# Weight pieces of a fused linear-attention and feed-forward kernel: fetched ahead of the second token group, with two of their sums done by accumulating transfers

## The chip, the cores and the metric

The kernel runs on one core of one Trainium2 chip. The metric is device time in microseconds (us) of one execution; lower is better. Engines are named as the profile names them: PE (TensorE matmuls), PEld (its weight loads, which overlap PE), DVE (VectorE), ACT (ScalarE), POOL (GpSimd) and SP (SyncE, which here only issues transfers). Each engine works through its own list of instructions in order, and waits where an instruction's inputs aren't there yet. Transfers are issued from the queues of SP, ACT or POOL and carried by 16 DMA engines.

## The reference

A decayed linear attention over 768 tokens, 4 batches, 8 heads of width 48, whose output (3,072 tokens of 384 values) goes through a feed-forward network with an exact GELU. The feed-forward weights are float64, the rest float32.

```python
for t in range(S):                                   # attention, per batch and head
    state = alpha[:, :, t, :, None] * state + np.einsum('bhd,bhe->bhde', k[:, :, t], v[:, :, t])
    y[:, :, t] = np.einsum('bhd,bhde->bhe', q[:, :, t], state)
x = y.transpose(0, 2, 1, 3).reshape(B * S, H * D)    # 3072 x 384
h = x @ w_in                                         # 384 -> 2048
g = 0.5 * h * (1.0 + erf(h * inv_sqrt2))
out = g @ w_out                                      # 2048 -> 384
```

## The kernel before

**Groups and units.** The tokens are cut into 12 groups of 256. A group's attention is done in two units, each for four heads: unit (g, u) is half u of group g. For a unit, DVE scans the decays forward and multiplies q by them (`ahead`, lines 254 to 258), scans them backward and multiplies k (lines 265 and 268); PE makes the scores and turns k over (lines 284 and 293); DVE masks the scores (line 305), ACT copies the turned k out (`kn`, line 300); PE multiplies with v (lines 322 and 340); DVE adds four states in a row (lines 357 and 359); PE adds the part that comes through the states (line 384, "the outer part" below); ACT and then PE and ACT again (groups 0 to 2) or DVE (later groups) split the result into a high and a low part of x (lines 426, 435, 441, 430). The bank `ybank` that holds a unit's result exists once, so units follow each other through it. After a group's second unit, small transfers finish x (line 450).

**Feed-forward steps.** The 2,048 hidden values are cut into 8 slices f. Step (g, f) is one first product for group g (`hp`, line 458, 18 matmuls of 256 columns), two GELUs on ACT (lines 470 and 471), the low part of the GELU's result, and one second product (`acc`, line 497, 12 matmuls of 384 columns). The low part is a DVE subtraction (line 476), or, for groups 0 to 2 in the first part of the program, a matmul with a negative identity (line 480) and an ACT copy (line 484). There are 96 steps. When steps of another group follow, the sums leave PSUM into `part` (lines 511 to 515, on DVE).

**Weight pieces.** Slice f needs two pieces, number 2f of `w_in` and 2f + 1 of `w_out`; 16 in all, each 128x768. [...] In the order of a piece n: `u` on ACT (line 197), then on DVE four operations c0 to c3 (lines 201, 205, 215, 220), which leave the leading bits in `w` and the rest; c4 (line 230) adds the two; `hi` (line 233, ACT) rounds the sum to the matmul's format, and `lo` (line 236, DVE) is what the rounding left. Steps with slice f can start once hi and lo of both pieces are there.

**What sets the order.** Nothing is ordered by a scheduler at run time. The kernel holds a small planner: operations with assumed costs, dependencies and ranks are placed on a simulated clock, and the list sorted by start is then issued to every engine by hand. Two things feed it that the change touches: the string `ORDER`, which interleaves units (digits) and pieces (letters), and dependency lists such as that of a piece's fetch. Units and pieces therefore stand in fixed order in each engine's list, and a list stops where its next instruction must wait. SP fetches the loads of units and pieces in its own order. POOL holds only set-up, 18 multiplications of q (line 261, groups 3 to 11) and 11 output transfers (line 521).

The two lines of the kernel before that the change replaces by transfers are these:

```python
nc.vector.tensor_tensor(out=d["w"], in0=d["w"], in1=staged[n].bitcast(F32)[:, 1::2], op=ALU.add)      # c4
nc.vector.tensor_tensor(out=flat(lo), in0=d["w"], in1=flat(hi).bitcast(F32), op=ALU.subtract)         # lo
```

Of the kernel before, what the change touches and what calls it, by code (L numbers as in the profile page):

```python
# [20 lines left out]
STAGE = 3  # L21
# [4 lines left out]
UNTIL = 100.0  # L26
# [5 lines left out]
ORDER = "0 1 2 3 a b c d e f 4 5 g h i j k l m n o p"  # L32
# [3 lines left out]
def gla_then_gelu_ffn(ctx: ExitStack, tc: tile.TileContext, q, k, v, alpha, qg, kg, ag, w_in, w_out, out):  # L36
# [154 lines left out]
    def conversion(n):  # L191
# [3 lines left out]
        def scaled():  # L195
            d["u"] = stage.tile([P, 2 * DM], F32, tag="u", bufs=1, name=f"u_{n}")
            nc.scalar.activation(d["u"], staged[n].bitcast(F32)[:, 1::2], AF.Copy, scale=2.0**-112)
# [5 lines left out]
        def signed():  # L203
            d["w"] = stage.tile([P, 2 * DM], F32, tag="w", bufs=2, name=f"w_{n}")
# [14 lines left out]
        def rest():  # L219
            nc.vector.scalar_tensor_tensor(  # L220
                out=staged[n].bitcast(F32)[:, 1::2],
# [7 lines left out]
        def whole():  # L229
            nc.vector.tensor_tensor(out=d["w"], in0=d["w"], in1=staged[n].bitcast(F32)[:, 1::2], op=ALU.add)  # L230

        def high():
            nc.scalar.copy(flat(hi), d["w"])

        def low():
            nc.vector.tensor_tensor(out=flat(lo), in0=d["w"], in1=flat(hi).bitcast(F32), op=ALU.subtract)
# [255 lines left out]
    def gemm2(g, f, ghi, glo, acc, first, last, done, n0=None):  # L492
        for k in range(2):
            for t in range(2):
                for j in range(2):
# [11 lines left out]
        def evacuate():
            o = parts[0 if g == "s" else g % NSB]
            for t in range(2):
                if g in started:  # L510
                    nc.vector.tensor_tensor(out=o[:, t], in0=o[:, t], in1=acc[t], op=ALU.add)
                elif t == 1 and g == NG - 1:
# [3 lines left out]
                if g == NG - 1:  # L516
                    nc.sync.dma_start(out[g * G + t * C : g * G + (t + 1) * C, :], o[:, t])
# [124 lines left out]
    def plan_unit(n):  # L642
# [11 lines left out]
        d["load"] = op("SP", "load", lambda: load_data(g, u), [old.get("outer"), old.get("scores"), old.get("c0"), old.get("c1")] + ([unit[n - NB * NU].get("inside")] if old else []), rank=r - 30, lands=2.8)  # L654
# [13 lines left out]
        if g < NSB:  # L668
# [25 lines left out]
    def plan_piece(n):  # L694
# [234 lines left out]
```

## Time and profile before

| | us |
|---|---|
| three runs | 543.62, 539.23, 541.49 |
| their median | 541.49 |
| the profiled execution's own time | 538.57 |
| its span in the profile | 537.0 |

| engine | busy us | share of the span |
|---|---|---|
| PE | 511.0 | 95% |
| PEld | 495.7 | 92% |
| DVE | 302.4 | 56% |
| ACT | 210.1 | 39% |
| POOL | 38.6 | 7% |

The span is 1.6 us shorter than the execution's time. The page cuts the span into 40 slices of 13.4 us and gives the busy share of each in tenths; a shares-of-the-span table hides what these show, that PE and DVE are bound in different parts of the program:

```
PE   6667899999999999999999999999999999999995
DVE  8799999989996976878339145132131121211211
ACT  5347666655435444343243243233232222222221
PEclk9557999999999999999999999999999999999999
DMA  5838655432004423334022020010010000000001
```

A PE row's duration is modelled, since matmuls overlap; PEld, whose rows overlap less, is a second measure of how full PE is. PEclk is the clock that PE was granted, in tenths of full speed.

### The profile page before, as it was taken

What the parts mean: (1) busy time and instruction counts of PE and PEld (TensorE: products, weight loads), DVE (VectorE), ACT (ScalarE), POOL (GpSimd) and SP (SyncE); (2) the same over time, 40 slices, a digit from 0 to 9 for tenths busy, and PEclk for the clock granted to TensorE, in tenths of its full rate; (3) what the DMA queues carried; (4) which work ended last, traced back from release to release, by engine and by line L of the source; (5) the groups of instructions that cost most, each with busy time, mean ns of one, the idle gap of its engine ahead of it and who ended that gap; (6) DMA issues with size and microseconds to landing.
All of it is one profiled execution on the core that took longest, in us unless ns stands there. A gap on an engine that the chain in (4) does not pass through costs nothing.

```text
span 537.0 us, 13927 instructions
## 1 busy us (share of the span) xinstructions
PE 511.0 (95%) x5993; PEld 495.7 (92%) x5993; DVE 302.4 (56%) x558; ACT 210.1 (39%) x407; POOL 38.6 (7%) x51
## 2 busy tenths in 40 slices
PE   6667899999999999999999999999999999999995
PEld 6557889999999999999999999999999999999995
DVE  8799999989996976878339145132131121211211
ACT  5347666655435444343243243233232222222221
POOL 5000000000001210111001000000000000000000
PEclk9557999999999999999999999999999999999999
DMA  5838655432004423334022020010010000000001
GB/s 169 287 110 224 180 181 170 129 118 89 1 1 125 151 84 97 99 106 134 0 81 84 2 79 12 1 40 9 1 40 6 0 31 2 30 0 1 31 1 34
DMA packets 20722, 39.49 MB, mean 74 GB/s; under 512 B 4112, under 2 KB 7616, under 8 KB 20656
## 3 DMA queue, kind: packets, MB, share of 16 engines
q1 hardware_dynamic: 19136, 33.93, 21.1%
q0 software_dynamic: 1232, 4.33, 2.4%
q8 instruction: 49, 0.80, 0.7%
q10 hardware_dynamic: 288, 0.30, 0.2%
q14 instruction: 17, 0.14, 0.1%
HBM read 31.46 MB, written 4.72 MB: 67 GB/s over the span
## 4 chain that ended last, share of the span: by engine, by line
PE 86%; DVE 5%; issue 1%; DMA 1%; ACT 1%; SPq 0%
PE hp L458 38%; PE acc L497 37%; PE ybank L384 4%; PE ybank L322 2%; PE s L293 2%; PE s L284 2%; PE ybank L340 2%; DVE state L359 1%; DVE w L205 1%; DVE st L220 1%; DMA qd<-in_qg_dram 1%; DVE rp L265 1%; SPq L153 0%; DVE pp L254 0%; DVE u L215 0%
## 5 line engine op out<-in xcount | busy, mean ns | idle before, releaser
L458 PE MATMUL hp<-x,wih 128*128 128x256 f32 x1152 | 214.1, 285 | 0.0
L458 PEld LDWEIGHTS hp<-x,wih 128*128 128x128 f32 x1152 | 183.5, 192 | 1.1
L458 PE MATMUL hp<-x,wil 128*128 128x256 f32 x576 | 163.3, 284 | 0.0
L476 DVE TENSOR_TENSOR glo<-hp,ghi 128x512 fp32r<-128x512 f32 x87 | 59.9, 688 | 177.5 <-ACT hp L471 177.5
L470 ACT ACTIVATE ghi<-hp 128x512 fp32r<-128x512 f32 x96 | 57.5, 599 | 232.1 <-PE hp L458 231.9
L497 PE MATMUL acc<-woh,ghi 128*128 128x384 f32 x384 | 131.3, 342 | 0.0
L497 PE MATMUL acc<-wol,ghi 128*128 128x384 f32 x384 | 128.6, 335 | 0.0
L458 PEld LDWEIGHTS hp<-x,wil 128*128 128x128 f32 x576 | 110.7, 192 | 0.0
L497 PE MATMUL acc<-woh,glo 128*128 128x384 f32 x384 | 82.1, 334 | 0.0
L497 PEld LDWEIGHTS acc<-woh,ghi 128*128 128x128 f32 x384 | 72.4, 188 | 0.8
L497 PEld LDWEIGHTS acc<-wol,ghi 128*128 128x128 f32 x384 | 72.4, 189 | 0.0
L497 PEld LDWEIGHTS acc<-woh,glo 128*128 128x128 f32 x384 | 67.9, 188 | 0.0
L471 ACT ACTIVATE hp<-hp 128x512 f32<-128x512 f32 x96 | 57.1, 595 | 0.0
L261 POOL TENSOR_TENSOR qd<-qd,pp 128x512 f32<-128x512 f32 x18 | 23.2, 1288 | 224.3 <-DVE pe L255 133.3
L265 DVE TENSOR_TENSOR_SCAN rp<-ad,rp,top 128x255 f32<-128x255 f32 x48 | 36.6, 803 | 0.1
L384 PEld LDWEIGHTS ybank<-qd,state 48*48 48x48 f32 x704 | 23.0, 128 | 12.9 <-DVE state L359 9.5
L384 PE MATMUL ybank<-qd,state 48*48 48x64 f32 x704 | 26.7, 229 | 8.2 <-DVE state L359 8.2
L359 DVE TENSOR_TENSOR state<-ybank,state 128x96 f32<-128x96 f32 x80 | 20.5, 256 | 18.3 <-PE ybank L340 16.1
L254 DVE TENSOR_TENSOR_SCAN pp<-ad,top 128x256 f32<-128x256 f32 x48 | 30.3, 677 | 0.0
L300 ACT COPY kn<-s 128x512 f32<-128x512 f32 x24 | 14.1, 586 | 31.3 <-PE ybank L340 25.5
L521 POOL DMA_DIRECT2D out_dram<-part x11 | 8.3, 752 | 237.4 <-DVE part L515 162.4
L322 PEld LDWEIGHTS ybank<-ss,vn 64*64 64x64 f32 x768 | 14.6, 144 | 11.6 <-DVE ss L305 4.1
(74 smaller groups left out, 428.7 us busy)
## 6 DMA issues: line engine op xcount, KB each, us to landing
st<-in_moe_w_in_dram SPq DMA_DIRECT2D x8, 768.0 KB, 5.2
st<-in_moe_w_out_dram SPq DMA_DIRECT2D x8, 768.0 KB, 4.8
ad<-in_ag_dram SPq DMA_DIRECT2D x48, 96.0 KB, 2.4
kd<-in_kg_dram SPq DMA_DIRECT2D x48, 96.0 KB, 2.3
qd<-in_qg_dram SPq DMA_DIRECT2D x48, 96.0 KB, 3.1
vn<-in_v_dram SPq DMA_DIRECT2D x12, 384.0 KB, 4.3
out_dram<-part POOLq DMA_DIRECT2D x11, 384.0 KB, 3.2
x<-z SPq DMA_DIRECT2D x63, 32.0 KB, 3.0
```

Of the source, the lines that this page charges most:

```text
L254: nc.vector.tensor_tensor_scan(pp[:, i], at[:, i], top, MID, ALU.mult, ALU.min)
L261: nc.gpsimd.tensor_tensor(out=qt, in0=qt, in1=pp, op=ALU.mult)
L265: nc.vector.tensor_tensor_scan(rp[:, i, G - 2 :: -1], at[:, i, G - 1 : 0 : -1], top[:, 1:], rp[:, i, G - 1 :], ALU.mult, ALU.min)
L300: nc.scalar.copy(d["kn"], d["s"][:, :, 2 * C : 4 * C])
L322: nc.tensor.matmul(ybank[o, b, t : t + CS], lhsT=vn[r, c, e : e + DP], rhs=d["ss"][r, h, 2 * i + c, :], start=(i == 0 and c == 0), stop=(j ...
L359: d["chain"] = nc.vector.tensor_tensor(out=st[j + 1], in0=new, in1=st[j], op=ALU.add)
L384: ins = nc.tensor.matmul(ybank[r, b, t : t + CS], lhsT=states[u][j][r, i], rhs=d["qt"][r, i, j * CS : (j + 1) * CS], start=False, stop=Tru ...
L458: nc.tensor.matmul(hp[:, j, :], lhsT=a[:, j, i * P : (i + 1) * P], rhs=x[:, i, :], start=(j == 0 and i == 0 and n == 0), stop=(i == NK - 1 ...
L470: nc.scalar.activation(ghi, hp, AF.Gelu)
L471: nc.scalar.activation(hp, hp, AF.Gelu)
L476: nc.vector.tensor_tensor(out=glo, in0=hp, in1=ghi.bitcast(F32), op=ALU.subtract)
L497: nc.tensor.matmul(acc[t], lhsT=a[:, j, t * C : (t + 1) * C], rhs=w[:, j, :], start=(first and j == 0 and k == 0 and w is wo_hi[f]), stop= ...
```

## The change

Five things change together.

1. The fetches of pieces 0 and 1 are issued right behind the loads of group 0, ahead of group 1's (ranks of `load` and `get`). `ORDER` now puts pieces 0 and 1 between the units of group 0 and group 1, and spreads the next ones; further buffers change (`STAGE` 2 for the staged pieces, `u` has two buffers, `w` three), and c3 writes into `u`, so that a staged piece is free after c3.
2. c4 is no DVE addition any more, but a transfer on POOL's queue that adds `u` onto `w` in place.
3. lo is no DVE subtraction any more: ACT writes the negated, rounded sum into lo, and a second adding transfer on POOL's queue adds `w` onto it. ACT has one more operation for each piece (line 234 of the changed kernel).
4. The first emptying of the sums of groups 0 to 2 moves from DVE to ACT, and the matmul form of the GELU's low part is used in fewer steps (`UNTIL` 60 for 100): 2 in place of 9, the others go to DVE.
5. The last output half is issued from ACT's queue instead of SP's.

```diff
-STAGE = 3
+STAGE = 2
-UNTIL = 100.0
+UNTIL = 60.0
-ORDER = "0 1 2 3 a b c d e f 4 5 g h i j k l m n o p"
+ORDER = "0 1 a b 2 3 c d 4 5 e f g h i j k l m n o p"
...
         def rest():
             nc.vector.scalar_tensor_tensor(
-                out=staged[n].bitcast(F32)[:, 1::2],
+                out=d["u"],
...
         def whole():
-            nc.vector.tensor_tensor(out=d["w"], in0=d["w"], in1=staged[n].bitcast(F32)[:, 1::2], op=ALU.add)
+            nc.gpsimd.dma_start(d["w"], d["u"], accum_op=ALU.add)
 
         def high():
             nc.scalar.copy(flat(hi), d["w"])
+            nc.scalar.activation(flat(lo), d["w"], AF.Copy, scale=-1.0)
 
         def low():
-            nc.vector.tensor_tensor(out=flat(lo), in0=d["w"], in1=flat(hi).bitcast(F32), op=ALU.subtract)
+            nc.gpsimd.dma_start(flat(lo), d["w"], accum_op=ALU.add)
...
-                elif t == 1 and g == NG - 1:
+                elif g in EARLY or t == 1 and g == NG - 1:
                     nc.scalar.copy(o[:, t], acc[t])
...
-                    nc.sync.dma_start(out[g * G + t * C : g * G + (t + 1) * C, :], o[:, t])
+                    (nc.scalar if t else nc.sync).dma_start(out[g * G + t * C : g * G + (t + 1) * C, :], o[:, t])
...
-        d["get"] = op("SP", "fetch", lambda: fetch(n), [q3.get("c4")], rank=r - 30.5, lands=4.5)
-        d["u"] = op("ACT", "u", fns[0], [d["get"], p.get("c3")], rank=-0.5)
+        d["get"] = op("SP", "fetch", lambda: fetch(n), [q3.get("c3")], rank=-33.0 + n if n < STAGE else r - 30.5, lands=4.5)
+        d["u"] = op("ACT", "u", fns[0], [d["get"], wops.get(n - 2, {}).get("c4")], rank=-0.5)
...
-        d["c4"] = op("DVE", "c4", fns[5], [d["c3"]], rank=r)
+        d["c4"] = op("POOL", "c4", fns[5], [d["c3"]], rank=r, lands=2.6)
         d["hi"] = op("ACT", "hi", fns[6], [d["c4"]], rank=-0.4)
-        d["lo"] = op("DVE", "lo", fns[7], [d["hi"]], rank=r)
+        d["hi"].cost *= 2
+        d["lo"] = op("POOL", "c4", fns[7], [d["hi"]], rank=r, lands=2.6)
```

**The start, on ACT.** Names carry the unit or the piece: `kn_0_1` is the turned k of unit (0, 1), `u_0` the first operand of piece 0, `junk` a range check of the decays. Before, ACT's list runs, behind the set-up, so:

```order
L300 COPY kn_0_0_275<-s_0_0_245 128x512
L165 ACTIVATE junk_0_319,outside_116<-ad0_118,lo_b_110 128x512
L197 ACTIVATE u_0_321<-st_0_266 128x768
L165 ACTIVATE junk_1_323,outside_116<-ad0_118,hi_b_112 128x512
L300 COPY kn_0_1_353<-s_0_1_328 128x512
```

and now so:

```order
L197 ACTIVATE u_0_270<-st_0_213 128x768
L197 ACTIVATE u_1_272<-st_1_223 128x768
L301 COPY kn_0_0_277<-s_0_0_249 128x512
L165 ACTIVATE junk_0_314,outside_116<-ad0_118,lo_b_110 128x512
L165 ACTIVATE junk_1_318,outside_116<-ad0_118,hi_b_112 128x512
L301 COPY kn_0_1_363<-s_0_1_322 128x512
```

The copy of unit (0, 0) now stands behind both pieces' arrival; that of unit (0, 1) no longer has a piece directly ahead of it.

**POOL's list.** Before, the first instruction after set-up is a multiplication of q for unit (3, 0). Now transfers stand ahead of it and around it (`w` is a piece's sum, `wil` and `wol` the low halves of the input and output weights of a slice):

```order
L230 DMA w_4_816<-u_4_668 128x768
L230 DMA w_5_853<-u_5_739 128x768
L262 TENSOR_TENSOR qd1_124<-qd1_124,pp_3_0_914 128x512
L237 DMA wil2_170<-w_4_816 128x768
L262 TENSOR_TENSOR qd1_124<-qd1_124,pp_3_1_1000 128x512
L237 DMA wol2_186<-w_5_853 128x768
```

Two transfers for each piece have been added, and the multiplication of unit (3, 0) waits behind the sums of pieces 4 and 5.

**DVE ahead of the outer part of unit (2, 1).** The prediction speaks of this place. Before:

```order
L305 TENSOR_TENSOR ss_2_1_977<-s_2_1_935,mask_155 128x512
L220 SCALAR_TENSOR_TENSOR st_5_687<-st_5_687,u_5_904 128x768
L230 TENSOR_TENSOR w_5_958<-w_5_958,st_5_687 128x768
L254 SCALAR_TENSOR_TENSOR pp_3_0_1013<-ad1_122,top_114 128x256 x2
L255 TENSOR_SCALAR pe_3_0_1015<-pp_3_0_1013 128x2
L256 RECIPROCAL rp_3_0_1014<-pe_3_0_1015 128x2
L359 TENSOR_TENSOR state1_1_151<-ybank_159,state1_0_150 128x96
L359 TENSOR_TENSOR state1_2_152<-ybank_159,state1_1_151 128x96
L359 TENSOR_TENSOR state1_3_153<-ybank_159,state1_2_152 128x96
```

and now:

```order
L266 SCALAR_TENSOR_TENSOR rp_3_0_915<-ad1_122,rp_3_0_915,top_114 128x255 x2
L269 TENSOR_TENSOR kd1_123<-kd1_123,rp_3_0_915 128x512
L255 SCALAR_TENSOR_TENSOR pp_3_1_1000<-ad1_122,top_114 128x256 x2
L256 TENSOR_SCALAR pe_3_1_1002<-pp_3_1_1000 128x2
L257 RECIPROCAL rp_3_1_1001<-pe_3_1_1002 128x2
L477 TENSOR_TENSOR glo_1_0_1035<-hp_1_0_942,ghi_1_0_997 128x512
L201 TENSOR_SCALAR u_6_976<-u_6_976 128x768
L477 TENSOR_TENSOR glo_1_1_1054<-hp_1_1_978,ghi_1_1_1032 128x512
L205 SCALAR_TENSOR_TENSOR w_6_1058<-st_6_887,u_6_976 128x768
L215 TENSOR_SCALAR u_6_976<-w_6_1058 128x768
L220 SCALAR_TENSOR_TENSOR u_6_976<-st_6_887,u_6_976 128x768
L360 TENSOR_TENSOR state1_1_151<-ybank_159,state1_0_150 128x96
```

Ahead of the same three states (of which the second fence shows the first) now stand also the rest of unit (3, 0), the forward scan of (3, 1), piece 6 and two low parts (`glo`); the additions of line 230 and the subtractions of line 236 are gone from the list.

**PE at the same place.** Before, the second product of step (1, 1) (`acc0_1_0` fed by `ghi_1_1`) follows the first product of step (1, 2):

```order
L458 MATMUL hp_1_2_1082<-x1_638,wil2_170 128x256
L435 MATMUL ybank_159<-z2_1072,minus_104 128x128 x2
L435 MATMUL ybank_159<-x2_874,minus_104 128x128 x2
L497 MATMUL acc0_1_0_961<-woh1_177,ghi_1_1_1065 128x384
L497 MATMUL acc0_1_0_961<-wol1_185,ghi_1_1_1065 128x384
```

Now it follows the inner part of unit (2, 1), ahead of that unit's outer part and of step (1, 2):

```order
L498 MATMUL acc0_1_0_1039<-woh0_176,glo_1_0_1035 128x384 x2
L498 MATMUL acc1_1_0_1040<-woh0_176,glo_1_0_1035 128x384 x2
L323 MATMUL ybank_159<-ss_2_1_897,vn0_117 64x64 x16
L341 MATMUL ybank_159<-vn0_117,kn_2_1_889 64x48 x12
L498 MATMUL acc0_1_0_1039<-woh1_177,ghi_1_1_1032 128x384
```

The scores of unit (3, 0), which stood behind step (0, 2)'s first product, stand ahead of it in the same way, behind step (1, 1)'s first product.

More of the change, by code (lines that the diff above doesn't have):

```diff
@@ L203, in signed @@
         def signed():
-            d["w"] = stage.tile([P, 2 * DM], F32, tag="w", bufs=2, name=f"w_{n}")
+            d["w"] = stage.tile([P, 2 * DM], F32, tag="w", bufs=3, name=f"w_{n}")
             nc.vector.scalar_tensor_tensor(
@@ L503, in gemm2 @@
                         )
+        EARLY = tuple(range(NSB))
         if not last:
@@ L653, in plan_unit @@
         old = unit.get(n - NB * NU, {})
-        d["load"] = op("SP", "load", lambda: load_data(g, u), [old.get("outer"), old.get("scores"), old.get("c0"), old.get("c1")] + ([unit[n - NB * NU].get("inside")] if old else []), rank=r - 30, lands=2.8)
+        d["load"] = op("SP", "load", lambda: load_data(g, u), [old.get("outer"), old.get("scores"), old.get("c0"), old.get("c1")] + ([unit[n - NB * NU].get("inside")] if old else []), rank=-40.0 + n if n < 2 else r - 30, lands=2.8)
         d["scan"] = op("DVE", "scan", start, [d["load"], p.get("q"), p.get("back")], rank=r)
@@ L667, in plan_unit @@
         d["outer"] = op("PE", "outer", lambda: outside_part(g, u), [d["chain"]], rank=r)
-        if g < NSB:
+        if n < 4:
             for what in ("scores", "inside", "outer"):
@@ L698, in plan_piece @@
         r = piece_rank[n]
-        d["get"] = op("SP", "fetch", lambda: fetch(n), [q3.get("c4")], rank=r - 30.5, lands=4.5)
-        d["u"] = op("ACT", "u", fns[0], [d["get"], p.get("c3")], rank=-0.5)
+        d["get"] = op("SP", "fetch", lambda: fetch(n), [q3.get("c3")], rank=-33.0 + n if n < STAGE else r - 30.5, lands=4.5)
+        d["u"] = op("ACT", "u", fns[0], [d["get"], wops.get(n - 2, {}).get("c4")], rank=-0.5)
         d["c0"] = op("DVE", "c0", fns[1], [d["u"]], rank=r)
-        d["c1"] = op("DVE", "c1", fns[2], [d["c0"], wops.get(n - 2, {}).get("lo")], rank=r)
+        d["c1"] = op("DVE", "c1", fns[2], [d["c0"], wops.get(n - 3, {}).get("lo")], rank=r)
         d["c2"] = op("DVE", "c2", fns[3], [d["c1"]], rank=r)
         d["c3"] = op("DVE", "c3", fns[4], [d["c2"]], rank=r)
-        d["c4"] = op("DVE", "c4", fns[5], [d["c3"]], rank=r)
+        d["c4"] = op("POOL", "c4", fns[5], [d["c3"]], rank=r, lands=2.6)
         d["hi"] = op("ACT", "hi", fns[6], [d["c4"]], rank=-0.4)
-        d["lo"] = op("DVE", "lo", fns[7], [d["hi"]], rank=r)
+        d["hi"].cost *= 2
+        d["lo"] = op("POOL", "c4", fns[7], [d["hi"]], rank=r, lands=2.6)
     for n in range(2 * NF2):
@@ L712, in gla_then_gelu_ffn @@
         plan_unit(n)
-    steps, plan = [], []
+    steps, plan, evacuated = [], [], set()
     next_f = [0] * NG
@@ L762, in gemm1_op @@
                 prev["last"] = True
-                prev["evac"] = Op("DVE", "part", lambda p=prev: p["out"](), [prev["gemm2"]], rank=-2)
-                waiting["DVE"].append(prev["evac"])
+                again = prev["g"] >= NSB or prev["g"] in evacuated
+                evacuated.add(prev["g"])
+                prev["evac"] = Op("DVE" if again else "ACT", "part", lambda p=prev: p["out"](), [prev["gemm2"]], rank=-2)
+                waiting[prev["evac"].eng].append(prev["evac"])
             state["run"] += 1
```

2 lines of the change are left out of this document (1 added, 1 removed).

## The prediction

> **What bounds the kernel now.** I read the shares in four stretches first. A row gives the stretch, its length, each engine's busy us with the number of instructions, PE's granted clock, the share of the 16 DMA engines, and GB/s.
>
> ```profile
> 0.00:44.00 44.00, 27.38 (x467) 25.03 (x467) 36.74 (x74) 19.99 (x37) 7.16 (x22) 0.66 0.62 192
> 44.00:77.00 33.00, 29.03 (x468) 26.53 (x467) 32.18 (x57) 21.86 (x42) 1.27 (x1) 0.94 0.62 185
> 77.00:160.00 83.00, 83.00 (x741) 81.52 (x740) 80.00 (x122) 44.22 (x76) 5.22 (x4) 1.00 0.30 93
> 160.00:532.00 372.00, 371.56 (x4325) 362.60 (x4323) 153.47 (x307) 123.91 (x256) 24.96 (x24) 1.00 0.15 45
> ```
>
> The columns are PE, PEld, DVE, ACT, POOL. From 77 us on PE is full (83.00 of 83), so what comes later can shorten only if PE has less to do. Between 44 and 77 us DVE is full instead (32.18 of 33), and PE has 4.0 us idle by its matmul rows, 6.5 us by its weight loads. The chain of work that ended last says the same in time order (start, us, what):
>
> ```profile
> 50.59 0.56 DVE u L201
> ...
> 52.19 0.54 DVE wil L236
> ...
> 57.07 1.28 DVE pp L254 x2
> 58.37 0.18 DVE pe L255
> ...
> 64.80 1.40 DVE rp L265 x2
> 66.22 0.69 DVE kd L268
> ...
> 68.25 0.93 DVE part L515 x2
> ...
> 75.16 0.27 DVE state L359
> 75.48 1.10 PE ybank L384 x32
> 77.00 1.07 PE hp L458 x9
> ```
>
> From 50.6 to 75.4 us it is on DVE without a break of another engine, through decoding of weights (lines 201 to 236), scans and emptying of sums; then the outer part of unit (2, 1) is released and PE runs full. So the reader is to see one place where time can be won: the front, before 77 us, and there DVE's list.
>
> **The change, part by part.** The durations (engine, shape, count, then total us and mean ns, or min/median/max):
>
> ```profile
> L230 DVE TENSOR_TENSOR w<-w,st x16: 946/958/959, 33.0 to 150.5; 128x768 f32<-128x768 f32 x16
> L236 DVE TENSOR_TENSOR wil<-w,wih x8: 948/952/2016, 35.4 to 143.7; 128x768 fp32r<-128x768 f32 x8
> L205 DVE SCALAR_TENSOR_TENSOR w<-st,u x16: 943/950/961, 28.9 to 146.7; 128x768 int32<-128x768 int32 x16
> L220 DVE SCALAR_TENSOR_TENSOR st<-st,u 128x768 f32<-128x768 uint16 x16 | 15.3, 957 | 0.4
> L476 DVE TENSOR_TENSOR glo<-hp,ghi 128x512 fp32r<-128x512 f32 x87 | 59.9, 688 | 177.5 <-ACT hp L471 177.5
> L233 ACT CAST wih<-w x8: 833/835/853, 34.0 to 142.2; 128x768 fp32r<-128x768 f32 x8
> ```
>
> *DVE's list in the front.* I count what stands ahead of the state that releases the outer part of unit (2, 1). Gone are six additions of line 230 (pieces 0 to 5) and five subtractions of line 236 (pieces 0 to 4): 11 x 0.955 = 10.5 us, and the emptying of the sums of line 515, 1.0 us (0.93 on the chain). New ahead of it are the four steps of piece 6 (line 201 0.56 by the chain, line 215 of the same kind and size as much, 0.95 and 0.96 by these rows: 3.0), the backward half of unit (3, 0) (1.40 + 0.69 = 2.1), the forward scan of (3, 1) (1.28 + 0.18 + about 0.2 = 1.6) and two low parts on DVE (2 x 0.69 = 1.4): 8.1 us. Net 11.5 - 8.1 = 3.4 us earlier. DVE has no other engine to hide behind there (32.18 of 33), so all of this lies on the path.
>
> *PE's list at that place.* Ahead of step (1, 2) PE now also does the second product of step (1, 1) and the scores of unit (3, 0), which would otherwise come after it:
>
> ```profile
> 79.55 2.14 PE acc L497 x12
> ...
> 83.99 0.69 PE L284 MATMUL s<-qd,kd 48*64 48x64 f32 x32
> 85.03 0.42 PE L497 MATMUL acc<-woh,ghi 128*128 128x384 f32 x1
> ```
>
> That is 2.1 and 1.0 us (83.99 to 85.03), 3.1 us of work moved from the full stretch into the stretch with gaps. It counts only where PE has gaps left: with the stretch 3.4 us shorter, 4.0 - 3.4 = 0.6 us by matmul rows, 6.5 - 3.4 = 3.1 us by weight loads. Between 0.6 and 3.1 I take the middle, 1.9.
>
> *The start.* The copy of unit (0, 0) moves behind the decoding of both first pieces on ACT, and SP fetches these ahead of group 1.
>
> ```profile
> 8.00 0.42 SPq L157 DMA_DIRECT2D vn<-in_v_dram  x1
> 11.30 0.58 ACT L300 COPY kn<-s 128x512 f32<-128x512 f32 x1 [4.41 <-PE s L293]
> 13.92 0.68 DVE L305 TENSOR_TENSOR ss<-s,mask 128x512 f32<-128x512 f32 x1
> 21.24 0.89 ACT L197 ACTIVATE u<-st 128x768 f32<-128x768 f32 x1 [8.52 <-DMA st<-in_moe_w_in_dram]
> 23.34 0.69 DVE L305 TENSOR_TENSOR ss<-s,mask 128x512 f32<-128x512 f32 x1 [3.48 <-ACT kn L300]
> ...
> st<-in_moe_w_in_dram SPq DMA_DIRECT2D x8, 768.0 KB, 5.2
> out_dram<-part POOLq DMA_DIRECT2D x11, 384.0 KB, 3.2
> ```
>
> Piece 1's fetch leaves SP at about 8.9 us (the load ahead at 8.00, then two of 0.42), lands 5.2 later at 14.1, u takes 0.9 and the copy 0.6: done at 15.6 in place of 11.9. Before, the mask that needs it began at 13.9 us, so DVE waits about 1.7 us more. Queued behind the copy are ACT's range checks, which nobody waits for soon, and the next copy. On the other side the wait of 3.48 us in the last DVE row goes: there the copy of unit (0, 1) stood behind u of piece 0, which waited 8.52 us for its fetch. Now that copy is free of it. Group 1's loads come about 1 us later per two fetches, but DVE takes group 1 only behind pieces 0 and 1, some 6 us of work; hidden, and if that cover were gone it would cost that 1 us. Sum between -3.5 and +1.7; I take 0, since these are idle times and the new list may wait at its own places.
>
> *Later matmuls, and the last output.* Seven of nine products with the negative identity go; in the full stretch that is five (77 us onwards).
>
> ```profile
> 81.52 0.39 PE L480 MATMUL hp<-ghi,minus 128*128 128x512 f32 x1
> 81.75 0.40 PE L458 MATMUL hp<-x,wih 128*128 128x256 f32 x2
> ...
> 531.83 0.84 SPq L517 DMA_DIRECT2D out_dram<-part x2
> ```
>
> The next matmul starts 0.23 us behind such a one, so -1.2 us; DVE gets five low parts as 0.69 us each instead, hidden by PE's own step (2.1 us for a second product above, as much for a first). The last output's second issue leaves SP's queue, where it stood 0.42 us behind the first; ACT itself makes that half a little later than DVE the other, so -0.2.
>
> *Added on ACT.* A negation for each piece, taken as long as line 233's cast: between 44 us and the end of the front five (4.2 us) and one emptying of sums (1.0), less two low parts that DVE now makes (two casts, about 1.2): 25.9 us of 29.6 in place of 21.86 of 33. Worse than the time is that `hi` waits for a transfer, with GELUs and x's casts queued behind it, for which PE waits. No row shows such a wait. It costs at least 0, and at most one landing (3.2 us, the row of the output transfers) that nothing covers; further ones meet a PE with work in store. ACT has slack, so nearer to 0: +0.5.
>
> *Added on POOL and the DMA engines.* 32 transfers of 384 KB. The issues take 0.75 us each (24 us) on an engine that is busy 7%; behind them in POOL's list stand the multiplications of q, covered as long as transfers don't queue. Their share of the DMA engines is in no row. The nearest rows are these, with the packets' time as a share of 16 engines' span:
>
> ```profile
> q1 hardware_dynamic: 19136, 33.93, 21.1%
> q0 software_dynamic: 1232, 4.33, 2.4%
> L521 POOL DMA_DIRECT2D out_dram<-part x11: 725/748/885, 169.5 to 500.9; - x11
> ```
>
> Below: an output transfer has the same size and queue, 0.024 x 537 / 11 = 1.2 us. Above: an adding one reads two operands, so count it as 768 KB of loads: 0.211 x 537 / 33.93 = 3.3 us per MB, 2.6 us. I take 1.8, between them, as only one of its two sides doubles. By 160 us, where the weights must be in, 28 of them fall behind 44 us: 50 us. Used there already are 0.62 x 33 + 0.30 x 83 = 45 us of 116. 95 of 116 fits: no cost. The two round trips of about 3.2 us put 5 us into each piece's chain, but pieces follow each other every 7.5 us (c4's first and last start: (150.5 - 33.0) / 15 = 7.8), so it costs nothing while each piece is done in its turn.
>
> Sum: -3.4 - 1.9 + 0 - 1.2 - 0.2 + 0.5 = -6.2 us. The profiled execution took 538.57, which gives 532.4; it lies 2.9 below the median of the three runs, 541.49, and against that median I predict 535.3, say 535.
>
> **Rivals.** *Slower: the adding transfers fill the DMA engines.* Free are 116 - 45 = 71 us; 71 / 28 = 2.5 us per transfer is the point from which this decides, just inside the bounds above. At 3.0 us the 28 need 84, 13 us too much, PE starves between 80 and 160 us by that, and the gain in the front cannot be cashed: 541.5 + 13, less 1.4 for the matmuls dropped, 553. For it: loads and additions would share engines that are 62% taken in the front, and the weight loads in the view of 8 to 50 us took 5.9 against 5.2 over all:
>
> ```profile
> st<-in_moe_w_in_dram SPq DMA_DIRECT2D x3, 768.0 KB, 5.9
> ```
>
> Against: the same-sized output takes 1.2. The Trainium skill speaks for this rival: "DMA: Bandwidth & Descriptors", section "Issuing engines are not separate DMA queues", says that transfers of all queues run on the same 16 engines, so that POOL's queue adds no bandwidth. The trace agrees as far as 5.9 against 5.2 shows it.
>
> *No change: ACT paces the front.* If `hi` stands 1 us for its landing at each of pieces 1 to 5 with the GELUs behind it, 5 us of the 6.2 go: 540. For it: ACT would be busy 25.9 of 29.6 us. Against: 21.86 of 33 leave it 11 us before.
>
> *No change: PE's clock falls back.* These are stretches around the first product:
>
> ```profile
> 30.00:40.00 10.00, 6.18 (x128) 5.72 (x128) 9.78 (x17) 4.51 (x11) 0.00 (x0) 0.50 0.47 140
> 44.00:48.00 4.00, 4.00 (x21) 4.00 (x20) 3.90 (x7) 2.17 (x4) 0.00 (x0) 0.52 0.87 266
> 48.00:52.00 4.00, 3.04 (x104) 2.27 (x103) 3.83 (x9) 3.63 (x6) 0.00 (x0) 1.00 0.59 147
> ```
>
> With PE busy in bits the clock is 0.50; only the unbroken first product lifts it. If a new wait drops it for 10 us, PE loses 5 us of work: 540. The Trainium skill, "TensorE: Matmul & The Clock Gate", section "HAM oscillation", puts the limit at idle gaps of about 3.4 us; the trace agrees so far as it rises within such a time here.
>
> *More gain:* PE's moved work counts whole (-3.1) and the wait of 3.48 goes without a new one: -10, 531.
>
> **How the numbers follow.** A measurement of this kernel tells about 1% (5.4 us) from no change. The forecast (-3 to -9) has 0.54, of which 0.42 are beyond 1%; more gain 0.08; ACT 0.13; clock 0.05; slower 0.20. So faster 0.50, same 0.12 + 0.18 = 0.30, slower 0.20. The range leaves out the far part of the slow rival (transfers above 2.8 us) and little below: 528 to 549; the forecast's own is 532 to 539.
>
> **What would show it.** Right: step (1, 2)'s first product starts near 73 us, DVE still full before it, PE full behind it, POOL's transfers landing within about 4 us. Wrong: landings of 6 us and more with a DMA share near 1 between 44 and 160 us and PE idle there; ACT idle ahead of line 233 for its transfer while PE idles; a granted clock of 0.5 behind 50 us; DVE idle in the front.

## The result, and the profile after

| kernel | median us (runs) | profiled execution | span | mean granted clock |
|---|---|---|---|---|
| before | 540.36 (539.18 to 543.62) | 538.57 | 537.0 | 0.967 |
| after | 560.90 (559.25 to 564.83) | 564.83 | 563.2 | 0.944 |

The changed kernel is slower: 1.0392 times the time before, 95% interval 1.0352 to 1.0432. The prediction was 535.

The same stretches of the changed kernel (stretch, its length, busy us and instructions of PE, PE's weight loads, DVE, ACT and POOL, PE's granted clock, share of the DMA engines, GB/s):

```profile
0.00:44.00 44.00, 22.71 (x388) 20.24 (x392) 31.05 (x62) 20.59 (x36) 10.89 (x26) 0.63 0.79 217
44.00:77.00 33.00, 25.76 (x415) 23.39 (x409) 25.06 (x51) 17.60 (x33) 5.13 (x7) 0.71 0.75 184
77.00:160.00 83.00, 69.93 (x693) 67.61 (x694) 58.51 (x97) 43.48 (x77) 21.18 (x22) 0.94 0.84 202
160.00:557.00 397.00, 396.45 (x4502) 387.40 (x4501) 161.72 (x323) 136.79 (x276) 29.16 (x29) 1.00 0.18 48
```

DVE was relieved as planned: 25.06 us in place of 32.18 between 44 and 77 us, 58.51 in place of 80.00 up to 160. PE got nothing for it. It is idle 13 of 83 us where it was full, and its clock falls to 0.71 between 44 and 77 us. The share of the DMA engines rises from 0.30 to 0.84 between 77 and 160 us. Behind 160 us PE is full as before, so the loss is made in front of that.

How much was lost shows in the matmuls of the two weight products. The rows give PE's busy time and matmuls of one line: of the kernel before, line 458 (first product, 18 to a step) and then line 497 (second product, 12 to a step).

```profile
0.00:77.00 77.00, 11.43 (x74) 10.97 (x75) 0.78 0.62 189
77.00:160.00 83.00, 41.23 (x324) 40.37 (x323) 1.00 0.30 93
...
0.00:77.00 77.00, 7.03 (x36) 6.18 (x36) 0.78 0.62 189
77.00:160.00 83.00, 39.61 (x211) 36.10 (x212) 1.00 0.30 93
```

The same two lines of the changed kernel, 459 and 498:

```profile
0.00:77.00 77.00, 6.50 (x37) 6.14 (x38) 0.67 0.78 203
77.00:160.00 83.00, 34.35 (x252) 33.48 (x252) 0.94 0.84 202
...
0.00:77.00 77.00, 5.68 (x24) 5.29 (x24) 0.67 0.78 203
77.00:160.00 83.00, 30.60 (x151) 27.50 (x152) 0.94 0.84 202
```

By 160 us the changed kernel has made 289 first-product matmuls in place of 398, and 175 second-product ones in place of 247: six steps fewer. Behind 160 us the kernel before spends 172.53 / 1332 x 18 = 2.33 us on a first and 170.88 / 907 x 12 = 2.26 on a second product (rows of the same two views for 160 to 570 us), so six steps are 27.5 us. The span grew by 26.2; the medians differ by 20.5, as the profiled execution is the longest of the four. About 2.2 us of it are no work of the change: the copy of unit (0, 0) on ACT begins at 18.59 us, in a run with the same list up to there (few_bytes, below) at 16.43, and the first adding transfer is issued only at 23.3.

Where it waits, by ACT's waits before 180 us (what waited for what: us in total, times, longest us):

```profile
ACT u L197 <- DMA w<-u: 16.9, 5, 5.0
ACT wih L233 <- DMA w<-u: 13.1, 5, 6.0
...
ACT woh L233 <- DMA w<-u: 5.0, 2, 3.6
```

That is 35.0 us in which ACT stands for an adding transfer of line 230: the casts (18.1 us) for the sum that it brings, u (16.9 us) for the buffer that it still reads. The page's queue row for POOL's queue (packets, MB, share of the 16 engines' span) and the landings (`st` is a piece as fetched; KB each, median us from issue to landing):

```profile
q0 software_dynamic: 5840, 16.91, 14.5%
...
st<-in_moe_w_in_dram SPq DMA_DIRECT2D x8, 768.0 KB, 6.2
st<-in_moe_w_out_dram SPq DMA_DIRECT2D x8, 768.0 KB, 9.6
w<-u POOLq DMA_DIRECT2D x16, 384.0 KB, 8.2
```

Of the 16 engines an adding transfer took (14.5% x 563.2 - 2.4% x 537.0) / 32 = 2.15 us, where the prediction took 1.8. It lands 8.2 us behind its issue. The fetches of w_out land in 9.6 us, before in 4.8.

One place shows the mechanism. ACT's list at the first product of the changed kernel (start, us, engine and line, what, and in brackets the idle time before it with what ended it):

```profile
50.27 0.19 ACT L165 ACTIVATION_READ_ACCUMULATOR junk<-ad,hi_b 128x1 f32 x1
55.62 0.83 ACT L233 CAST wih<-w 128x768 fp32r<-128x768 f32 x1 [5.16 <-DMA w<-u]
56.36 0.84 ACT L234 ACTIVATE wil<-w 128x768 fp32r<-128x768 f32 x1
57.22 1.28 ACT L471 ACT_TABLE_LOAD   x1
58.51 0.60 ACT L471 ACTIVATE ghi<-hp 128x512 fp32r<-128x512 f32 x1
59.01 0.59 ACT L472 ACTIVATE hp<-hp 128x512 f32<-128x512 f32 x1
```

And PE beside it:

```profile
52.75 0.28 PE L459 MATMUL hp<-x,wil 128*128 128x256 f32 x1
52.87 0.40 PE L436 MATMUL ybank<-x,minus 128*128 128x256 f32 x2
59.65 0.80 PE L481 MATMUL hp<-ghi,minus 128*128 128x512 f32 x1 [6.39 <-ACT hp L472]
60.38 1.14 PE L323 MATMUL ybank<-ss,vn 64*64 64x64 f32 x32
```

The first product is done at 53 us. Its GELU could start then, but in ACT's list the cast of piece 2 stands ahead of it and waits 5.16 us for a transfer. So PE is idle for 6.39 us, and what follows runs at half clock (1.14 us for the inner products that took 0.69 before).

A second place, at 137 us, has the same form. Here the emptying of the sums, which the change moved to ACT, stands behind the cast; first ACT, then PE:

```profile
137.37 0.83 ACT L233 CAST wih<-w 128x768 fp32r<-128x768 f32 x1 [5.97 <-DMA w<-u]
138.11 0.84 ACT L234 ACTIVATE wil<-w 128x768 fp32r<-128x768 f32 x1
138.85 0.84 ACT L515 COPY part<-acc 128x384 f32<-128x384 f32 x2
...
139.37 0.69 PE L498 MATMUL acc<-woh,ghi 128*128 128x384 f32 x1 [4.87 <-ACT part L515]
```

In both waits the DMA engines are full, though their mean share from 77 to 160 us is 0.84:

```profile
51.00:55.60 4.60, 2.26 (x13) 2.06 (x12) 4.50 (x10) 0.00 (x0) 0.80 (x1) 0.82 1.07 269
130.00:137.00 7.00, 4.50 (x33) 4.29 (x31) 6.83 (x13) 1.09 (x2) 1.31 (x2) 1.00 1.02 213
```

A third gap of PE, 4.77 us up to 107.19, ends with small transfers x<-z. ACT's share of them stands behind a u that waited 5.03 us, but SP's share also left only at 100.78 us, so that gap can't be put on ACT alone.

### The profile page after: what moved, and what is told of

Its sections match the earlier page's. It is cut to its first block, busy times and chain, and to the rows that moved or that the text cites. A ratio compares the mean times of both kernels' runs of the same rounds, so it can differ in the third digit from the quotient of the medians.

```text
span 563.2 us, 14004 instructions
## 1 busy us (share of the span) xinstructions
PE 515.6 (92%) x5986; PEld 499.1 (89%) x5986; DVE 276.9 (49%) x531; ACT 218.9 (39%) x422; POOL 66.4 (12%) x83
## 3 DMA queue, kind: packets, MB, share of 16 engines
q0 software_dynamic: 5840, 16.91, 14.5%
## 4 chain that ended last, share of the span: by engine, by line
PE 74%; DMA 14%; issue 5%; ACT 2%; DVE 2%; POOL 1%; SPq 0%; POOLq 0%; ACTq 0%; DVEq 0%
PE hp L459 32%; PE acc L498 31%; DMA w<-u 9%; PE ybank L385 3%; PE ybank L323 2%; PE s L294 2%; PE ybank L341 2%; PE s L285 2%; DMA ad<-in_ag_dram 2%; DMA st<-in_moe_w_out_dram 2%; DMA x<-z 1%; DMA wil<-w 1%; ACT kd L107 1%; DVE u L220 1%; DVE w L205 0%
## 5 line engine op out<-in xcount | busy, mean ns | idle before, releaser
L477 DVE TENSOR_TENSOR glo<-hp,ghi 128x512 fp32r<-128x512 f32 x94 | 64.8, 689 | 210.4 <-ACT hp L472 206.2
L498 PE MATMUL acc<-woh,ghi 128*128 128x384 f32 x384 | 132.9, 346 | 5.4 <-ACT part L515 4.9
L498 PE MATMUL acc<-wol,ghi 128*128 128x384 f32 x384 | 129.9, 338 | 0.0
L498 PEld LDWEIGHTS acc<-wol,ghi 128*128 128x128 f32 x384 | 73.6, 192 | 0.0
L360 DVE TENSOR_TENSOR state<-ybank,state 128x96 f32<-128x96 f32 x80 | 20.5, 257 | 26.7 <-PE ybank L341 24.5
L323 PEld LDWEIGHTS ybank<-ss,vn 64*64 64x64 f32 x768 | 14.9, 148 | 17.2 <-DVE ss L306 9.1
L323 PE MATMUL ybank<-ss,vn 64*64 64x64 f32 x768 | 18.4, 240 | 12.2 <-DVE ss L306 8.8
```

Of the source, the lines that this page charges most:

```text
L323: nc.tensor.matmul(ybank[o, b, t : t + CS], lhsT=vn[r, c, e : e + DP], rhs=d["ss"][r, h, 2 * i + c, :], start=(i == 0 and c == 0), stop=(j ...
L360: d["chain"] = nc.vector.tensor_tensor(out=st[j + 1], in0=new, in1=st[j], op=ALU.add)
L477: nc.vector.tensor_tensor(out=glo, in0=hp, in1=ghi.bitcast(F32), op=ALU.subtract)
L498: nc.tensor.matmul(acc[t], lhsT=a[:, j, t * C : (t + 1) * C], rhs=w[:, j, :], start=(first and j == 0 and k == 0 and w is wo_hi[f]), stop= ...
```

## The experiments

All runs in one table. "Ratio" is to runs of the kernel before on the same chip. "Landing" is the median of w<-u in us, "ACT" its waits for w<-u before 180 us, in us.

| kernel | us | ratio, 95% interval | landing | ACT |
|---|---|---|---|---|
| after | 560.9 | 1.0392 (1.0352 to 1.0432) | 8.2 | 35.0 |
| few_bytes | 538.4 | 0.9964 (0.9934 to 0.9994) | 4.8 | 5.5 |
| half_columns | 551.8 | 1.0195 (1.0147 to 1.0242) | 6.4 | 21.0 |
| plain | 549.8 | 1.0180 (1.0115 to 1.0245) | 6.3 | 17.2 |
| order_alone | 551.2 | 1.0199 (1.0135 to 1.0263) | - | - |
| both_on_dve | 540.6 | 1.0017 (0.9999 to 1.0035) | - | - |
| low_on_dve | 556.6 | 1.0296 (1.0228 to 1.0364) | 6.9 | 47.2 |
| low_told | 544.6 | 1.0079 (1.0049 to 1.0109) | 7.5 | 19.8 |
| low_few | 538.1 | 0.9946 (0.9920 to 0.9972) | 4.6 | 19.4 |
| sum_on_dve | 542.2 | 1.0040 (1.0006 to 1.0074) | - | - |
| sum_told | 545.8 | 1.0101 (1.0070 to 1.0132) | - | - |
| told | 555.7 | 1.0274 (1.0228 to 1.0320) | 7.5 | 17.9 |
| told_loaded | 548.8 | 1.0156 (1.0107 to 1.0205) | 8.0 | 6.2 |
| three_u | 562.5 | 1.0371 (1.0321 to 1.0421) | 8.2 | 23.2 |
| fetch_first | 539.0 | 0.9975 (0.9942 to 1.0007) | - | - |
| first_and_last | 540.0 | 0.9999 (0.9974 to 1.0023) | - | - |
| until_only | 546.0 | 1.0105 (1.0068 to 1.0141) | - | - |
| small_parts | 545.4 | 1.0099 (1.0061 to 1.0137) | - | - |
| front_low | 540.4 | 0.9999 (0.9970 to 1.0028) | - | - |

### Is it the bytes, the round trips, or the order?

**few_bytes**, the changed kernel's order and waits with 4 KB in each transfer (8 of 768 columns; the sums of the others are left out):

```diff
-            nc.gpsimd.dma_start(d["w"], d["u"], accum_op=ALU.add)
+            nc.gpsimd.dma_start(d["w"][:, :8], d["u"][:, :8], accum_op=ALU.add)
-            nc.gpsimd.dma_start(flat(lo), d["w"], accum_op=ALU.add)
+            nc.gpsimd.dma_start(flat(lo)[:, :8], d["w"][:, :8], accum_op=ALU.add)
```

> The order, the waits and the 32 issues of the changed kernel stay; each adding transfer carries 8 of 768 columns, so the sums are left out but for those. Theory BYTES (the additions fill the DMA engines, landings stretch to 8 us and PE waits for them): landings of w<-u fall from a median of 8.2 us to 4 or less, the share of the DMA engines between 77 and 160 us falls from 0.84 to near 0.3, and the time comes back to 537 to 543 us. Theory TRIP (the round trip itself, with ACT's later instructions queued behind the wait, costs it): landings stay near the smallest seen, 3.9 us, and at least two thirds of the loss remain, 553 to 561. Theory ORDER (the new order, its start above all, costs it): 556 to 561 whatever the landings do.

It took 538.4, 22.5 us less than the changed kernel: in this order the whole loss hangs on the bytes. TRIP as put here and ORDER are out. The landings fell to 4.8 us and the DMA share between 77 and 160 us to 0.42, both less far than BYTES had them (4 and 0.3), and PE is full again there:

```profile
77.00:160.00 83.00, 83.00 (x896) 81.05 (x897) 63.53 (x110) 49.83 (x89) 21.97 (x23) 1.00 0.42 112
...
w<-u POOLq DMA_DIRECT2D x16, 4.0 KB, 4.8
```

ACT's list at the first product is the same one, the wait in it is 1.24 us and not 5.16:

```profile
46.48 0.83 ACT L233 CAST wih<-w 128x768 fp32r<-128x768 f32 x1 [1.24 <-DMA w<-u]
47.22 0.84 ACT L234 ACTIVATE wil<-w 128x768 fp32r<-128x768 f32 x1
48.07 1.28 ACT L471 ACT_TABLE_LOAD   x1
49.37 0.60 ACT L471 ACTIVATE ghi<-hp 128x512 fp32r<-128x512 f32 x1
```

The Trainium skill, "DMA: Bandwidth & Descriptors", section "Issuing engines are not separate DMA queues", says that transfers of all queues share 16 engines. The trace agrees: SP's fetches of w_out land in 9.6 us beside the full transfers on POOL's queue and in 5.3 us in this run. The prediction's 5.9 against 5.2 could not show that, as nothing was on POOL's queue of the kernel before until 169.5 us.

**half_columns** does 384 of 768 columns in each transfer, **plain** leaves out `accum_op` (a copy of all 384 KB).

> The changed kernel, order and waits kept, each adding transfer over 384 of 768 columns (the sums of the others are left out). DMA time per transfer about 1.1 us, as with plain copies of the whole, which took 549.8. If the DMA engines' time is the quantity, 545 to 553, and landings about 6 us; if the loss sets in only where they fill up, 538 to 543.

> Each adding transfer becomes a plain copy of the same 384 KB on the same queue (the additions are left out; the order and waits stay). If the addition doubles the work of the DMA engines, a copy costs about the 1.2 us of an output transfer in place of 2.1, and by BYTES most of the loss goes: 540 to 549. If copying 384 KB within SBUF is as dear as adding, or by TRIP or ORDER: 555 to 562.

They took 551.8, inside its range, and 549.8, 0.8 above the range for a cheap copy (540 to 549) and 5 below the other one. POOL's queue rows, half_columns first:

```profile
q0 software_dynamic: 5840, 10.62, 9.3%
```

```profile
q0 software_dynamic: 4816, 16.91, 9.2%
```

By the same sum as above (12.9 us are the 2.4% of before) that is (9.3% x 551.0 - 12.9) / 32 = 1.20 us of the DMA engines for half an addition and (9.2% x 546.5 - 12.9) / 32 = 1.17 for a whole copy, against 2.15 for a whole addition and 0.22 for the one of 4 KB (3.7% of 535.4). So adding costs about what copying twice the bytes costs. Two quite different transfers with equal DMA time give equal landings (6.4 and 6.3 us) and nearly equal times. At the three sizes that were run (0.22, about 1.2 and 2.15 us of the DMA engines) the loss grows steadily, and no threshold shows: in the four runs with this one order, ACT's waits are 5.5, 17.2, 21.0 and 35.0 us and the times 538.4, 549.8, 551.8 and 560.9.

**order_alone** keeps the changed kernel's order and lets DVE make both sums at the places of the transfers:

```diff
-            nc.gpsimd.dma_start(d["w"], d["u"], accum_op=ALU.add)
+            nc.vector.tensor_tensor(out=d["w"], in0=d["w"], in1=d["u"], op=ALU.add)
-            nc.scalar.activation(flat(lo), d["w"], AF.Copy, scale=-1.0)
-            nc.gpsimd.dma_start(flat(lo), d["w"], accum_op=ALU.add)
+            nc.vector.tensor_tensor(out=flat(lo), in0=d["w"], in1=flat(hi).bitcast(F32), op=ALU.subtract)
```

> The order of the changed kernel, but both sums made by DVE at the places at which the transfers were issued; no adding transfers, no negation on ACT. BYTES and TRIP: no wait for a transfer beyond the weight fetches remains; DVE has about 28 x 0.95 us more to do in front of 160 us, where it was busy 58.5 + 25.1 of 116 us, so 538 to 546. ORDER: 553 to 561.

551.2, between the two ranges: the order costs, though less than the whole loss. The reading is that an order set for a DVE without sums is a bad one for a DVE with them, and the next run bears it out. **both_on_dve** has the same edit and tells the planner, so that it orders anew (`op("DVE", "c4", ...)` and `op("DVE", "lo", ...)` in place of the two on POOL):

> No adding transfers, both sums on DVE, and the planner knows it and orders anew; all else of the change stays (first fetches, two buffers of fetched pieces, five products fewer, emptying by ACT). The order kept with DVE's sums took 551.2. If that loss came from DVE's list being set for other work, a new order recovers it: 537 to 543. If the other parts of the change (the start, the shorter fetch-ahead) cost by themselves, it stays at 546 to 553.

540.6, no different from before. So the rest of the change, taken together, costs nothing and brings nothing (one part alone costs 6.8 us, until_only below, so parts can offset each other); order_alone's loss was its mismatch. The rest includes an edit that the list of five leaves out: the planner's higher costs for a unit's matmuls now hold for the first four units (`if n < 4`) in place of groups 0 to 2.

### Whose wait is it: the halves apart

**low_on_dve** undoes the transfer of the low half, **sum_on_dve** that of the sum; the planner knows in both. Each has 16 of the 32 transfers. ACT waits for the transfer of the sum (its cast reads the result, and the u of the piece two further on needs the buffer that is added), while the low half is read by PE alone.

> Only the sum of a piece by transfer (16 of them); the low half by DVE again, and no negation on ACT; the planner orders anew. BYTES: half of the additions' 60 us of DMA time goes, share about 0.6 between 77 and 160 us, time 540 to 549. TRIP: ACT still waits for each sum ahead of its cast, 550 to 558. ORDER: 555 to 561.

> Only the low half by transfer (16 of them, read by PE alone); the sum by DVE, so that ACT waits for no transfer; ordered anew. The bytes are those of the run with only the sum by transfer, 556.6. BYTES as one quantity: 552 to 558 again. WAIT (a stretched landing costs where ACT's list stands behind it): 539 to 547.

556.6, in the ranges of both TRIP and ORDER, and 542.2, as WAIT had it: the same bytes, 14 us apart. None of PE's waits before 180 us in sum_on_dve is for a low half. The two runs differ in their orders too, so low_told and low_few keep to the first of them. **low_told** then leaves low_on_dve as it is and tells the planner the landing that the trace showed:

```diff
-        d["c4"] = op("POOL", "c4", fns[5], [d["c3"]], rank=r, lands=2.6)
+        d["c4"] = op("POOL", "c4", fns[5], [d["c3"]], rank=r, lands=7.0)
-            bus[0] = max(bus[0], o.end) + (1.9 if o.lands > 4 else ...
+            bus[0] = max(bus[0], o.end) + (2.15 if o.lands == 7.0 else 1.9 if o.lands > 4 else ...
```

> Only the sum of a piece by transfer, as in the run of 556.6, with the planner told that it lands 7.0 us behind its issue (6.9 was its median there) and takes 2.15 us of the DMA engines. The bytes and landings stay; ACT's casts should stand where the transfer has landed. QUEUE (what costs is ACT's list standing behind a landing): ACT's waits for w<-u fall from 47 us before 180 to below 15, and the time to 539 to 547. CAPACITY or the length of a piece's chain: 552 to 558.

544.6, 12 us back with the same transfers, which land no earlier (7.5 us). ACT's waits, of low_on_dve:

```profile
ACT wih L233 <- DMA w<-u: 21.4, 6, 6.2
ACT woh L233 <- DMA w<-u: 14.8, 5, 4.1
```

and of low_told:

```profile
ACT u L197 <- DMA w<-u: 17.4, 8, 5.1
ACT wih L233 <- DMA w<-u: 2.4, 1, 2.4
```

But for one, the casts now stand where their sum has landed. The waits of u went up to 17.4 us, past the 15 expected for all of them, and cost little.

**low_few** is low_on_dve with 8 of 768 columns in each transfer; the sums of the other columns are left out.

> The order of the run with only the sum by transfer (556.6), with 8 of 768 columns in each transfer. If that order is harmless once landings are 3 to 5 us, 538 to 544. If the order is bad by itself, 548 to 557.

538.1. That order is harmless when the transfers land in 4.6 us. So what costs in low_on_dve is the stretched landing, not the order by itself. ACT still waits 19.4 us in low_few, as long as in low_told: the sum of the waits is no price, it depends on what stands behind each.

### With all 32 transfers

**told** and **told_loaded** do the same to the changed kernel, with `lands=3.9` (the smallest landing seen), and with 8.2 and 5.7 (the medians).

> The changed kernel, with the planner told what the trace shows: 2.15 us of the DMA engines for each adding transfer in place of 1.5, and a landing of 3.9 us in place of 2.6. If the loss is the mismatch of order and landings, ACT's waits for w<-u (30 us before 180 us) fall below 15 and the time to 545 to 552. If it is the DMA engines' capacity, an order can't mend it: 555 to 563.

> The changed kernel with all 32 transfers, the planner told the landings measured in it (8.2 us for the sum, 5.7 for the low half) and 2.15 us of the DMA engines for each. QUEUE: as with half the transfers, some 12 us or more come back, 541 to 549. CAPACITY (32 x 2.15 us beside the loads leave PE without weights, whatever the order): 553 to 561, with a share of the DMA engines above 0.85 between 77 and 160 us and PE idle there.

555.7 and 548.8. The first by itself spoke for CAPACITY, as 3.9 us is half of what the transfers then took (7.5). With the landings as measured, ACT's waits fall to 6.2 us and 12.1 of the 20.5 us come back, just within QUEUE's range. CAPACITY's sign came too: a share of 0.88 between 77 and 160 us, with PE idle for 4.2 us there. The rest, 10.4 us above few_bytes, has another face. The windows of told_loaded:

```profile
44.00:52.00 8.00, 6.93 (x88) 6.32 (x88) 7.76 (x17) 3.86 (x6) 0.85 (x1) 0.50 1.08 268
52.00:60.00 8.00, 7.09 (x160) 6.25 (x159) 7.66 (x15) 7.72 (x15) 1.72 (x2) 0.99 1.03 262
60.00:68.00 8.00, 5.50 (x78) 4.97 (x69) 7.04 (x15) 3.35 (x9) 3.00 (x4) 0.65 1.00 202
68.00:77.00 9.00, 9.00 (x136) 8.49 (x136) 5.61 (x12) 6.42 (x12) 2.17 (x2) 0.93 0.98 256
```

The DMA engines are full for these 33 us (1.08 to 0.98), and everything that goes through them is late, the small transfers too: the median of x<-z on SP's queue (32 KB, which PE's first product waits for) is 5.6 us between 15 and 160 us, against 3.2 in few_bytes. This order with 4 KB in each transfer was not run, so how much of the 10.4 us is the full engines and how much the new order stays open, and so does whether an order exists that hides it.

**three_u** gives the changed kernel a third buffer for u, so that u waits for the transfer three pieces back:

```diff
-            d["u"] = stage.tile([P, 2 * DM], F32, tag="u", bufs=2, name=f"u_{n}")
+            d["u"] = stage.tile([P, 2 * DM], F32, tag="u", bufs=3, name=f"u_{n}")
-        d["u"] = op("ACT", "u", fns[0], [d["get"], wops.get(n - 2, {}).get("c4")], rank=-0.5)
+        d["u"] = op("ACT", "u", fns[0], [d["get"], wops.get(n - 3, {}).get("c4")], rank=-0.5)
```

> The changed kernel with a third buffer for u, so that the first step of a piece waits for the adding transfer three pieces back, not two. QUEUE: ACT's waits of line 197 for w<-u (17 us before 180) go, and a third to a half of the loss with them: 549 to 555. CAPACITY: 557 to 563.

562.5, nothing gained; the expectation of QUEUE was wrong here, and the time lies in CAPACITY's range. u's waits of 16.9 us are gone altogether, but the casts wait 23.2 us in place of 18.1, and PE stands at the same place:

```profile
PE hp L481 <- ACT hp L472: 7.0, 2, 6.5
```

At this place the wait that matters is that of the cast ahead of the GELU; a freed u only moves up to it.

### The smaller terms

**fetch_first** is the kernel before with the change's ranks for the first loads and fetches alone; **first_and_last** adds the last output's issue by ACT.

> The kernel before with the loads of unit (0, 0) and (0, 1) and the fetches of pieces 0 and 1 at the head of SP's list as in the change; nothing else. The prediction's term for the start is 0, between -3.5 and +1.7: 535.9 to 541.2. If the start costs what the later mask shows (kn(0, 0) behind u of piece 1, 5 us later), 542 to 545.

> The kernel before with the first fetches moved ahead (538.97 against 539.83 alone) and the last output's second issue by ACT (a term of -0.2): 538.3 to 539.2, ratio 0.996 to 0.999.

0.9975, within the term's range, and 0.9999, above what was expected: neither can be told from no change.

**until_only** is the kernel before with `UNTIL = 60.0`; **small_parts** adds the emptying by ACT and the last output's issue.

> The kernel before, with products with the negative identity only before 60 us of the plan. The term: -1.2, so 538.5 to 539.5 against 540.3, if PE keeps its clock in the front. Together with the emptying by ACT it took 545.4, with PE's clock back at 0.5 from 56 to 70 us: if that came with the fewer products' new order, 543 to 547 again, and the clock shows it; if with the emptying by ACT, the term's 539.

> The kernel before, with three small parts of the change alone: products with the negative identity only before 60 us of the plan, first emptying of the sums of the first batch by ACT, and the last output's second half issued by ACT. The prediction's terms give -1.2 - 0.2 and up to -1.0 for DVE: 536.9 to 538.1 against 539.3; if they are worth nothing, 539 to 540.

546.0 and 545.4, both slower than the terms had it, and not by one cause. In until_only PE's clock dips less than its expectation named (0.79 from 52 to 60 us, before 1.00). But DVE has the low parts and the sums, and up to 160 us PE is busy 134.73 us in place of 139.41, with holes where it was full (stretches of 10 us):

```profile
130.00:140.00 10.00, 8.86 (x62) 8.36 (x60) 9.83 (x15) 5.21 (x8) 0.00 (x0) 1.00 0.26 84
140.00:150.00 10.00, 8.89 (x85) 8.56 (x86) 9.90 (x16) 3.87 (x7) 0.00 (x0) 1.00 0.33 115
```

In small_parts PE loses its clock from 56 to 70 us; the kernel before was busy 3.80 + 2.36 of the 8 us from 52 to 60 and kept 1.00 there:

```profile
52.00:56.00 4.00, 1.94 (x45) 1.49 (x39) 3.26 (x8) 1.45 (x4) 0.00 (x0) 0.91 0.76 228
56.00:60.00 4.00, 4.00 (x26) 3.86 (x23) 3.90 (x7) 2.17 (x5) 0.00 (x0) 0.50 0.39 96
60.00:70.00 10.00, 9.26 (x114) 8.65 (x114) 7.57 (x14) 2.65 (x6) 0.00 (x0) 0.55 0.50 163
```

**front_low** (low halves of pieces 0 to 5 by transfer, all else on DVE) and **sum_told** (sum_on_dve with `lands=4.8` and 2.15) were tries for a faster version.

> A candidate: the low halves of pieces 0 to 5 by transfer, all other sums by DVE. With all 16 low halves by transfer 120 products were done by 77 us against 110 before, and the lead was lost at 80 to 90 and 110 to 120 us, where PE had gaps. If those gaps came from the later transfers, the lead of 10 products (1.4 us) stays: 536.5 to 539. If not, 540 to 543.

> Only the low halves by transfer, as in the run of 542.2, with the planner told 4.8 us to land and 2.15 us of the DMA engines each. PE's gaps at 80 to 90 and 110 to 120 us (3.6 us together) should close if it orders its products for the landings: 537 to 540. If the order was not what made them, 541 to 544.

540.4 and 545.8, both misses: no gain, and in sum_told a worse order from better numbers. So an order that the planner makes anew can be off by several us for no reason of its own, and part of the 12 us in low_told and in told_loaded may be of that kind; the rows of ACT's waits say that it is not all. No run that computes everything was measurably faster than the kernel before.

## Why the prediction was wrong, step by step

**The step that failed** is the last one of the DMA part: "95 of 116 fits: no cost", and with it "two round trips of about 3.2 us ... so it costs nothing while each piece is done in its turn". Three things in it:

- The size was off a little: 2.15 us per transfer in place of 1.8, 60 us in place of 50 for the 28. With it the sum reads 105 of 116 and still "fits". So the size alone did not mislead.
- The test was the wrong one. An average share below 1 does not say that a transfer lands on time. The landing rose from 4.8 to 6.3 and 8.2 us as the mean share between 77 and 160 us rose from 0.42 to 0.66 and 0.84, and the engines were full where it mattered (1.07 and 1.02 in the two waits above). A landing of 3.2 us was taken from output transfers that all run behind 169 us, and the plan itself stood on 2.6 us (`lands=2.6` in the diff).
- A piece was seen as a chain of its own, with 7.8 us until the next one. But ACT takes its list in order: the cast that waits for the sum holds up the GELU of another step, and PE waits for that. "At most one landing (3.2 us)" bounded what in the trace are twelve waits on the casts and u of up to 6.0 us, 35.0 in all. The +0.5 for ACT was the term with the largest error: telling the plan the landings took 12.1 us off.

**DVE's list, -3.4.** DVE was relieved, but the gain did not come even without the bytes: few_bytes has 109 matmuls of the two products done by 77 us, before 110. The outer part of unit (2, 1), which was to start 3.4 us earlier than at 75.48 us, starts at 79.18 in few_bytes and at 90.38 in the changed kernel; PE goes into it without a gap in both, so DVE no longer releases it. "All of this lies on the path" was wrong: DVE was full, but when it is freed ACT's list is next. There the cast and the new negation stand ahead of the first GELU, and PE waits 2.88 us for it (50.50 us) where the kernel before has a gap of 0.94; its clock is 0.50 from 52 to 56 us. That order was read in few_bytes and not changed by itself.

**PE's moved work, -1.9.** It could only pay in a shorter front, and there was none. In few_bytes step (1, 2)'s first product starts at 80.21 us, 3.2 later than before, with the 3.1 us of moved work ahead of it: level. In the changed kernel it starts at 91.40, where 73 was the sign of being right.

**The start, 0.** Right for the ranks of the first loads by fetch_first. In the changed kernel the copy of unit (0, 0) begins at 18.59 us, where the term had it done at 15.6, because piece 1's u begins at 17.80 and not at 14.1, and the first mask moves from 13.92 to 19.27. Chance has a part in it: in few_bytes the copy begins at 16.43, in both_on_dve at 17.05. That part was not run by itself; both_on_dve, in which PE waits 7.2 us for a mask in the same way, is level with before as a whole.

**Five products fewer, -1.2.** Alone it costs 6.8 us (until_only against its own runs of before): "hidden by PE's own step" leaned on a DVE that was busy 80.00 of 83 us there. The plan also made another order of it, and how much of the 6.8 us that is was not shown. In the changed kernel, where the sums are off DVE, the term can't be read apart.

**The last output, -0.2.** Too small to be seen.

**The rivals.** The slow one was the right one, with its sign and its landings, but its mechanism was capacity from 2.5 us per transfer on. At the measured 2.15 it would have said no loss. The runs put up to 12 us on ACT's list behind stretched landings (told_loaded against after) and leave some 10, of which full engines are the likely cause; that second half is argued and not shown. "ACT paces the front" had the right queue and priced it at 5 us; "PE's clock falls back" happened as well, in the 6.39 us gap. In that gap the three are one chain, and they were given as separate cases with separate chances.

Of the signs named ahead, those for wrong came: landings of 6 us and more with PE idle, ACT idle ahead of line 233, a clock of 0.5 behind 50 us, and DVE idle in the front (25.06 of 33 us busy).

## What to carry to other kernels

Work moved from an engine to a transfer is priced by its landing under load and by who stands behind it in an in-order list, not by whether the DMA engines' time fits on the average: look for the instruction that will wait for the landing, and what is queued behind it. Give a result by transfer to a reader that comes to it late (here PE, for which no wait for a low half shows: 542.2), not to one that reads it at once with other engines' work queued behind (556.6). And when a planner sets the order, its durations are part of the change: the same transfers cost some 12 us less once their measured landing was in the plan, though such an order also moves by some us on its own.

## What the hardware showed that was not expected

- In this kernel an adding transfer within SBUF of 384 KB took 2.15 us of all 16 DMA engines, a plain copy of the same bytes 1.17, an addition of half as many 1.20.
- A transfer of 4 KB by POOL's queue still took 2.3 to 4.8 us to land (medians of wol<-w and w<-u in few_bytes) and 0.22 us of the engines; POOL spent 0.85 us on issuing an adding transfer and 0.54 on a plain one.
- PE's clock went back to 0.5 behind idle gaps of 2.88 us (few_bytes, 47.6 to 50.5) and of 1.88 us amid part-time work (small_parts, 53.6 to 55.5); by the rows of PE's weight loads the gaps are 3.09 and 2.02 us. The Trainium skill, "TensorE: Matmul & The Clock Gate", section "HAM oscillation", speaks of idle gaps above about 3.4 us; these two are shorter, and the measurement decides. The prediction's "the trace agrees" rested on how fast the clock rises, which says nothing about gaps.
